# Attention and two expert layers on one core: first keys loaded once, and TensorE's hand-over matmuls of the set-up written a step earlier

## The chip, the core and the metric

The kernel runs on one core of a Trainium2 chip. A core has five engines that each take their instructions in the order in which they are written and wait for one another by semaphores: TensorE (PE in the profile; PEld its weight loads), VectorE (DVE), ScalarE (ACT), GpSimd (POOL) and Sync (SP), which here issues loads and stores. The metric is the device time of one execution in microseconds.

## The reference

Three layers follow one another: attention over pooled keys and values, a product layer, and a layer of eight experts with one chosen per token.

```python
k_p = k.reshape(B, H, Sp, pool, D).mean(axis=3)       # pool = 8; 8 x 8 heads, 576 x 64
v_p = v.reshape(B, H, Sp, pool, D).mean(axis=3)
scores = scale * np.matmul(q, k_p.transpose(0, 1, 3, 2))
...                                                   # softmax over the 72 pooled keys
return np.matmul(attn, v_p).astype(np.float32)
...
a = x @ w1                                            # 4608 tokens, 512 -> 1024
b = x @ w2
h = a * b @ w3
return (h @ w_out).astype(np.float32)
...
logits = x @ w_gate + modality_bias[modality_id]
h = np.maximum(x[mask] @ w1[e], 0.0)                  # mask: the tokens of expert e
out[mask] = gate_w[mask, None] * (h @ w2[e])
```

## The kernel before

**Precision.** The weights come as 64-bit numbers. A *conversion* of a piece (`step(n)`, L401) makes two 32-bit parts of it: ScalarE takes the next piece apart (`conv_a`, L391 and L393) and rounds the high part of this one (L408), VectorE puts the bits of the next one together (`conv_b`, L398 and L399), and GpSimd subtracts (`sub_pool`, L117) for the low part. A product is made of three matmuls (`mm3`, L112 to L114): high by high, high by low, low by high. Results of attention are split in the same way: ScalarE copies the high part out of PSUM, VectorE subtracts.

**Set-up** (`set_up`). The product of w3 and w_out (with the gate's weights worked in as extra columns) is made once, in two passes of eight *folds* (`fold_mm`, twelve matmuls each). A loop over rounds j = 0 to 7 makes the first pass: two conversions, then a fold. In rounds 2 to 5 it also writes the attention scores of one tile of 128 tokens: score matmuls (L263), VectorE's maxima and differences (L275, L277), the exponential on ScalarE, the sums and the normalisation. The keys pooled for it (`prep_k`, L177) come in through `load_k`. The second loop, again of eight folds, has one conversion for each fold and, by a table of hooks that run behind the fold (`more`), the first half's way out of PSUM, the sums of the values (`V1`), the transposes of the attention weights (`T`), their product with the values (`V`), and the gate's weights: `turn` transposes them, `mul` multiplies, `back` transposes the result and stores it as columns 256 to 259.

**First chunk** (`first_chunk`, chunk 0 of 9). `mm1` runs over m = 0 to 7: 24 matmuls against w1 and w2, then a times b on ScalarE and VectorE. Hooks with a key `(m,)` run before that product of a and b, hooks with key m behind it. They hold the conversions of the weights of m + 2, the scores of the next chunk, and the second half's gate. `mm_w` (L629) follows. From the second chunk on `next_chunk` runs, which has no conversions.

All engines' instructions are issued in the order of the code. PSUM has buffers by tag: four for `mm`, two for `tp`, one pair for `sc`; a matmul into a buffer waits until the last reader of what stood there is done. SBUF tiles go by tags in the same way (`st2` has two).

Of the kernel before, what the change touches and what calls it, by code (L numbers as in the profile page):

```python
# [22 lines left out]
P = 128  # L23
# [64 lines left out]
def _program(outer, tc, nc, I, out):  # L88
# [159 lines left out]
    def softmax_parts(t):  # L248
# [43 lines left out]
        return exps, norm, (ex, ext)  # L292

    def attn_T(exs, j, ps_of, t):
        if j < 4:
# [3 lines left out]
            nc.scalar.copy(t[:, 0], ps)  # L299
            nc.vector.tensor_tensor(t[:, 1], ps, t[:, 0].bitcast(F32), op=ALU.subtract)  # L300
            return t
        kn, lo = slice(0, 6 * TK), slice(2 * TK, 4 * TK)
        for n in range(2):
# [3 lines left out]
            nc.scalar.copy(t[kn, n], ps[kn])  # L307
            nc.vector.tensor_tensor(t[lo, n], ps[lo], t[lo, n].bitcast(F32), op=ALU.subtract)
        return t

    def attn_V(a, z, aT, xh, xl, ps_of):
        kn = slice(0, 6 * TK)
        for pr in range(4):
# [3 lines left out]
            nc.scalar.copy(xh[:, pr, a:z], ps)  # L317
            nc.vector.tensor_tensor(xl[:, pr, a:z], ps, xh[:, pr, a:z].bitcast(F32), op=ALU.subtract)
# [8 lines left out]
    aT0 = []  # L327

    class Attention:
# [19 lines left out]
        def S(self, i):  # L349
            self.K(i)  # L350
            for f in self.S3(i):
                f()

        def S3(self, i):
# [5 lines left out]

        def T(self, js):
            for j in js:
                t = aT0[j] if self.ch == 0 and j < 4 else st4("aT", (P, 2, 512), F32R)
                self.aT[j] = attn_T(self.ex, j, mm_ps if self.ch == 0 else tp_ps, t)
# [6 lines left out]
        def V(self):  # L371
            if not self.segs:
                return
# [3 lines left out]
            attn_V(a, z, self.aT, *self.x, mm_ps)  # L377
            if self.segs:
                need(prep_v2, self.segs[0][2])

# [92 lines left out]
    def w_gate(W, wf, ps_of):  # L473

        wT = {}
        g = []

        def turn(nb):
            tps = ps_of("wtp")
            for k in range(4):  # L480
                nc.tensor.transpose(tps[:, P * k:P * k + P], wf[:, k, P * nb:P * nb + P], ident)
            wT[nb] = st2("wT")
            nc.scalar.copy(wT[nb], tps)

        def mul(nb):
            if nb == 0:
                g.append(ps_of("wgp"))
            nc.tensor.matmul(g[0][:E], lhsT=wg[:, nb], rhs=wT[nb], start=nb == 0, stop=nb == 3)

        def back():  # L490
            gT = st2("gT", (E, 512))
            nc.scalar.copy(gT, g[0][:E])
            gp = ps_of("wgt")[:, :32].rearrange("p (k a b) -> p k a b", k=4, a=2)
            for k in range(4):
                nc.tensor.transpose(gp[:, k].rearrange("p a b -> p (a b)"), gT[:, P * k:P * k + P], ident[:E, :E])
            nc.scalar.copy(W[0][:, :, :, 256:260], gp)
            nc.vector.tensor_tensor(W[1][:, :, :, 256:260], gp, W[0][:, :, :, 256:260].bitcast(F32), op=ALU.subtract)
        return turn, mul, back
# [6 lines left out]
    def set_up():  # L505
# [497 lines left out]
```

## Time and profile before

| | us |
|---|---|
| median of 3 runs | 1357.05 |
| lowest, highest | 1353.14, 1358.21 |
| the profiled execution | 1350.23 |
| its span | 1348.5 |
| TensorE busy | 1234.3 (92%) |
| VectorE, GpSimd, ScalarE busy | 677.7, 402.3, 369.7 |

The profile is of one execution. Times in it count from the start of the span; the busy time of an engine is the time in which it had an instruction in work. Matmuls are pipelined: the distance between two starts is what one costs, not its own duration. The granted clock is 1.00 where TensorE has 2.4 GHz; over a stretch it is a mean between its two levels, 1.2 and 2.4 GHz.

### The profile page before, as it was taken

The page shows a single profiled execution, that of the slowest core. Times are in us where ns is not written, and L with a number is a line of the kernel's source. Part 1 is how long each engine was busy: PE and PEld are TensorE (multiplying, and loading weights), DVE is VectorE, ACT ScalarE, POOL GpSimd, SP SyncE. Part 2 cuts the span into 40 slices and gives each one's busy share as a digit, 9 for nine tenths or more (in the row PEclk, how much of TensorE's full clock was granted, in tenths as well). Part 3 has the DMA queues.
Part 4 walks back from the last instruction along what each step waited for, and adds up shares of the span by engine and source line. Part 5 has one row for each costly group of instructions (what it writes and reads, how often), then busy time and mean ns, then how long its engine had stood idle before and what let it go on. Part 6 is the DMA issues. An engine that isn't in the chain of part 4 may idle for free. (4 is left out here: it accounts for less than half of the span.)

```text
span 1348.5 us, 17452 instructions
## 1 busy us (share of the span) xinstructions
PE 1234.3 (92%) x6518; PEld 1046.4 (78%) x6518; DVE 677.7 (50%) x1325; ACT 369.7 (27%) x717; POOL 402.3 (30%) x464
## 2 busy tenths in 40 slices
PE   1566777799999999999999999999999999999997
PEld 1454546788989898898989889797888888888886
DVE  3574466554454545445453443465635565565452
ACT  2353454222222232323223222222121122212121
POOL 1361134014050231405023110314533443344142
PEclk8887888899999999999999999999999999999999
DMA  8502243130301203030020100224513441443240
GB/s 342 175 21 83 78 127 116 44 118 16 111 31 60 82 15 118 11 113 29 25 83 13 36 1 32 94 95 154 190 63 148 172 159 54 172 172 119 102 167 20
DMA packets 53165, 126.71 MB, mean 94 GB/s; under 512 B 12656, under 2 KB 12912, under 8 KB 53040
## 3 DMA queue, kind: packets, MB, share of 16 engines
q1 hardware_dynamic: 45680, 105.63, 22.5%
q0 software_dynamic: 7232, 19.71, 3.7%
q8 instruction: 57, 0.93, 0.3%
q14 instruction: 52, 0.43, 0.1%
q10 hardware_dynamic: 144, 0.02, 0.0%
HBM read 105.36 MB, written 20.55 MB: 93 GB/s over the span
## 5 line engine op out<-in xcount | busy, mean ns | idle before, releaser
L112 PE MATMUL w<-xh,w 128*128 128x512 f32 x576 | 231.8, 402 | 4.8 <-ACT w L408 1.9
L114 PE MATMUL w<-xh,w 128*128 128x512 f32 x576 | 227.2, 394 | 1.4 <-POOL w L117 1.4
L113 PE MATMUL w<-xl,w 128*128 128x512 f32 x576 | 226.4, 393 | 0.0
L289 POOL TENSOR_TENSOR ex<-ex,sm 128x576 f32<-128x576 f32 x36 | 41.7, 1159 | 391.2 <-PE sc L263 263.6
L112 PEld LDWEIGHTS w<-xh,w 128*128 128x128 f32 x576 | 109.6, 190 | 28.0 <-DVE asb L613 2.1
L114 PEld LDWEIGHTS w<-xh,w 128*128 128x128 f32 x576 | 109.3, 190 | 26.2 <-POOL w L117 2.7
L112 PE MATMUL e<-xh,e1h 128*128 128x512 f32 (+2 forms) x320 | 121.5, 380 | 5.7 <-issue 4.6
L113 PEld LDWEIGHTS w<-xl,w 128*128 128x128 f32 x576 | 109.7, 190 | 21.2
L113 PE MATMUL e<-xl,e1h 128*128 128x512 f32 (+2 forms) x320 | 122.6, 383 | 0.0
L114 PE MATMUL e<-xh,e1l 128*128 128x512 f32 (+2 forms) x320 | 121.1, 378 | 0.1
L114 PE MATMUL e<-e2h,abl 128*128 128x512 f32 x296 | 117.1, 395 | 3.0 <-DVE abl L813 3.0
L112 PE MATMUL e<-e2h,abh 128*128 128x512 f32 x296 | 117.8, 398 | 0.5 <-DVE abl L813 0.5
L629 PE MATMUL x2ps<-Wh,abh 128*128 128x260 f32 x576 | 118.2, 286 | 0.0
L629 PE MATMUL x2ps<-Wl,abh 128*128 128x260 f32 x576 | 116.7, 283 | 0.0
L113 PE MATMUL e<-e2l,abh 128*128 128x512 f32 x296 | 116.1, 392 | 0.0
L629 PE MATMUL x2ps<-Wh,abl 128*128 128x260 f32 x576 | 116.0, 283 | 0.0
L613 DVE TENSOR_TENSOR asb<-asb,w 128x512 f32<-128x512 f32 x72 | 49.3, 684 | 114.1 <-PE w L114 63.5
L614 ACT CAST abh<-asb 128x512 fp32r<-128x512 f32 x72 | 44.7, 620 | 182.8 <-DVE asb L613 182.8
L812 ACT ACTIVATE abh<-e 128x512 fp32r<-128x512 f32 (+2 forms) x80 | 45.4, 567 | 168.2 <-PE e L114 142.2
L825 POOL DMA_INDIRECT out<-o,idc x37 | 37.5, 1014 | 180.3 <-ACT o L824 166.9
L629 PEld LDWEIGHTS x2ps<-Wh,abh 128*128 128x128 f32 x576 | 89.9, 190 | 0.3
L629 PEld LDWEIGHTS x2ps<-Wl,abh 128*128 128x128 f32 x576 | 89.8, 189 | 0.0
(187 smaller groups left out, 2216.3 us busy)
## 6 DMA issues: line engine op xcount, KB each, us to landing
raw<-ew_in SPq DMA_DIRECT2D x80, 512.0 KB
q<-q_in SPq DMA_DIRECT2D x36, 256.0 KB
x2d<-x SPq DMA_DIRECT2D x36, 256.0 KB
kr<-k_in SPq DMA_DIRECT2D x28, 288.0 KB
vr<-v_in SPq DMA_DIRECT2D x28, 256.0 KB
cv<-w_in SPq DMA_DIRECT2D x12, 512.0 KB
stage<-w_in SPq DMA_DIRECT2D x10, 512.0 KB
stage<-wo_in SPq DMA_DIRECT2D x6, 512.0 KB
```

The lines of the kernel that those rows point to most:

```text
L112: nc.tensor.matmul(ps, lhsT=wh, rhs=xh, start=start, stop=False)
L113: nc.tensor.matmul(ps, lhsT=wh, rhs=xl, start=False, stop=False)
L114: nc.tensor.matmul(ps, lhsT=wl, rhs=xh, start=False, stop=stop)
L289: nc.gpsimd.tensor_tensor(e3, e3, bc(sm.unsqueeze(2), [P, H, SP_]), op=ALU.mult)
L613: nc.vector.tensor_tensor(a, a, ps[1], op=ALU.mult)
L614: nc.scalar.copy(abh[:, m], a)
L629: nc.tensor.matmul(pss[hf][:, :260], lhsT=l[:, m, cols], rhs=r[m // 4][:, m % 4, hf], start=m == 0 and r is Wh and l is abh, stop=m == 7 a ...
L812: nc.scalar.activation(hT[0][:, m, :w], ps[:, :w], AF.Relu)
L825: nc.gpsimd.indirect_dma_start(out=out, out_offset=bass.IndirectOffsetOnAxis(idc[:, i, 0:1], 0), in_=o, in_offset=None, bounds_check=N - 1 ...
```

## The change

The keys of batch 0 are remembered, so `prep_k(0)` doesn't load them a second time. In the set-up and the first chunk the small matmuls whose results another engine then reads (scores, transposes of attention and of the gate's weights, product with the values, the gate's products) are taken apart from the reading part (`diff`, `split`, `keep`, `out`) and stand a round, a fold or a step ahead of it: `parts(j - 1)` writes the score matmuls ahead of fold j, and their maxima follow in round j + 1. In the second pass the tables `vec` (the reading parts) and `ten` (TensorE's parts) both run ahead of the fold. The four turns of the second half's gate get a PSUM buffer each (two of `tp`, two banks of `sc`) and SBUF tiles of the tag `raw`. Sums of the values and loads of chunk 1 stand one or two steps earlier in m.

```diff
-        if b == 0:
+        if b == 0 and b not in k_raw:
             kr = ab0["abh"].bitcast(F32)[:, :4 * S].rearrange("p (a s) -> p a s", a=4)
             for pr in range(4):
                 nc.sync.dma_start(kr[:, pr], I["k"][b, :, pr * S:(pr + 1) * S])
                 if pr == 0:
                     load_q(0)
-            return [kr[:, pr] for pr in range(4)]
+            k_raw[0] = [kr[:, pr] for pr in range(4)]
...
-        for v, m, e, sh in parts:
-            nc.vector.tensor_reduce(out=m, in_=v, op=ALU.max, axis=AX.X)
-        for v, m, e, sh in parts:
-            nc.vector.tensor_tensor(e, v, bc(m.unsqueeze(len(sh) - 1), sh), op=ALU.subtract)
+        def diff():
+            for v, m, e, sh in parts:
+                nc.vector.tensor_reduce(out=m, in_=v, op=ALU.max, axis=AX.X)
+            for v, m, e, sh in parts:
+                nc.vector.tensor_tensor(e, v, bc(m.unsqueeze(len(sh) - 1), sh), op=ALU.subtract)
...
+        def split(to, of, part):
+            nc.scalar.copy(to, of)
+            nc.vector.tensor_tensor(part[0], part[1], part[2].bitcast(F32), op=ALU.subtract)
...
+            return lambda: split(t[:, 0], ps, (t[:, 1], ps, t[:, 0]))
...
-        def S3(self, i):
+        def parts(self, i):
...
+        def T2(self, js):
+            steps = []
+            for j in js:
+                t = self.aT[j] = aT0[j] if self.ch == 0 and j < 4 else st4("aT", (P, 2, 512), F32R)
+                steps.append(attn_T(self.ex, j, mm_ps if self.ch == 0 else tp_ps, t))
+            return steps
...
-            wT[nb] = st2("wT")
-            nc.scalar.copy(wT[nb], tps)
...
+        def keep(nb):
+            wT[nb] = wt_of()
+            nc.scalar.copy(wT[nb], tps[nb])
...
+            g.append(st2("gT", (E, 512)))
+            nc.scalar.copy(g[1], g[0][:E])
+
+        def back2():
+            gp = ps_of[5]("wgt")[:, :32].rearrange("p (k a b) -> p k a b", k=4, a=2)
+            g.append(gp)
...
+        def out():
+            nc.scalar.copy(W[0][:, :, :, 256:260], g[2])
+            nc.vector.tensor_tensor(W[1][:, :, :, 256:260], g[2], W[0][:, :, :, 256:260].bitcast(F32), op=ALU.subtract)
...
-        s3 = None
+        sm = {}
         for j in range(8):
-            if 2 <= j < 6:
-                att.K(j - 2)
-                s3 = att.S3(j - 2)
+            now = sm.get(j - 2)
+            if now:
+                now[0]()
             step(2 * j)
-            if s3:
-                s3[0]()
+            if now:
+                now[1]()
             step(2 * j + 1)
-            if s3:
-                s3[1]()
-            s3 = None
-            fold_mm(accs, j)
+            if now:
+                now[2]()
             if j == 0:
                 att.K(0)
                 raw_load(11)
                 load_v0()
+            if 1 <= j < 5:
+                sm[j - 1] = att.parts(j - 1)
+            fold_mm(accs, j)
...
-        more = {0: [lambda: fold_out(accs, W[0], wf0, (0, 1))],
-                1: [lambda: fold_out(accs, W[0], wf0, (2, 3)), lambda: att.V1()],
-                2: [lambda: att.T((0, 1))],
-                3: [lambda: att.T((2, 3)), lambda: load_k(1)],
-                4: [lambda: att.T((4,)), lambda: turn(0), lambda: turn(1)],
-                5: [att.V, lambda: mul(0), lambda: mul(1)],
-                6: [lambda: turn(2), lambda: turn(3)],
-                7: [lambda: mul(2), lambda: mul(3), back]}
+        late = []
+        def end():
+            for f in late:
+                f()
+            late[:] = []
+        vec = {0: [lambda: fold_out(accs, W[0], wf0, (0, 1))], 1: [lambda: fold_out(accs, W[0], wf0, (2, 3))],
+               2: [end, lambda: att.V1()], 3: [end, lambda: load_k(1)], 4: [end, lambda: keep(0), lambda: keep(1)],
+               5: [end], 6: [lambda: keep(2), lambda: keep(3)]}
+        ten = {1: [lambda: late.extend(att.T2((0, 1)))], 2: [lambda: late.extend(att.T2((2, 3)))],
+               3: [lambda: late.extend(att.T2((4,))), lambda: turn(0), lambda: turn(1)],
+               4: [lambda: late.extend(att.V(True))],
+               5: [lambda: turn(2), lambda: turn(3), lambda: mul(0), lambda: mul(1)],
+               7: [lambda: mul(2), lambda: mul(3)]}
         for j in range(8):
             step(16 + j)
+            run(vec, j)
+            run(ten, j)
             fold_mm(accs2, j)
-            run(more, j)
         step(24)
+        back()
+        back2()
         step(25)
+        w_out()
...
+        sc2 = psum.tile([P, 2, 512], F32, name="wtp2", tag="sc", bufs=1)
+        bank = lambda i: lambda name: sc2[:, i]
+        gate = w_gate(W[1], wf1, [tp_ps, tp_ps, bank(0), bank(1), tp_ps, tp_ps],
+                      lambda: at.tile([P, 512], F32, name="wT", tag="raw", bufs=RAW))
...
-        turn, mul, back = gate
-        s3 = []
+        turn, keep, mul, back, back2, w_out = gate
+        sm = {}
         def scores(i):
             att.K(i)
-            s3[:] = att.S3(i)
-
-        h1 = {(m,): [lambda m=m: step(28 + 2 * m), lambda m=m: step(29 + 2 * m)] for m in range(6)}
+            sm[i] = att.parts(i)
+        h0 = {m: [lambda m=m: step(28 + 2 * m), lambda m=m: step(29 + 2 * m)] for m in range(6)}
+        h1 = {m: [] for m in range(8)}
+        h0[0][:0] = [lambda: turn(0), lambda: turn(1), lambda: turn(2), lambda: turn(3)]
+        h0[0].insert(5, lambda: need(prep_k, 1))
+        h1[0] += [lambda: keep(0), lambda: keep(1), lambda: keep(2), lambda: keep(3)]
+        h0[1][:0] = [lambda: mul(0), lambda: mul(1), lambda: mul(2), lambda: mul(3)]
+        h1[1] += [back, lambda: load_k(2)]
+        h0[2][:0] = [back2]
+        h1[2] += [w_out]
         for i in range(4):
-            h = h1[i + 1,]
-            h.insert(0, lambda i=i: scores(i))
-            h.insert(2, lambda: s3[0]())
-            h.append(lambda: s3[1]())
-        h1[(0,)].insert(0, lambda: need(prep_k, 1))
-        h1[0] = [lambda: turn(0), lambda: turn(1)]
-        h1[1] = [lambda: mul(0), lambda: mul(1), lambda: turn(2), lambda: turn(3)]
-        h1[2] = [lambda: mul(2), lambda: mul(3), lambda: load_k(2)]
-        h1[3] = [back]
-        h1[4] = [load_routing]
-        h1[5] = [lambda: early_v(1), prep_routing]
-        h1[6] = [att.V1, lambda: att.T((0, 1))]
-        h1[7] = [lambda: att.T((2, 3)), lambda: att.T((4,))]
+            h0[i + 1].insert(len(h0[i + 1]) - (2 if i == 0 else 4), lambda i=i: scores(i))
+            h1[i + 1] += [lambda i=i: sm[i][0]()]
+            h0[i + 2].insert(len(h0[i + 2]) - 1, lambda i=i: sm[i][1]())
+            h0[i + 2] += [lambda i=i: sm[i][2]()]
+        h1[4] += [load_routing, lambda: early_v(1)]
+        h0[6] = [prep_routing]
+        h1[5] += [att.V1]
+        h1[6] += [lambda: att.T((0, 1))]
+        h1[7] += [lambda: att.T((2, 3)), lambda: att.T((4,))]
+        h1.update({(m,): h for m, h in h0.items()})
         ab = mm1(0, x, h1)
```

On TensorE, first pass: wps are the accumulators of the folds, f4 and f0 the operands of folds 0 and 1, f5 and f1 those of folds 2 and 3, and sc and scm the scores of tiles 0 and 1. Before:

```order
L114 MATMUL wps_146<-f4_108,f0_104 128x512
L263 MATMUL sc_233<-kblk0_87,q_121 128x144 x4
L112 MATMUL wps_143<-f5_109,f1_105 128x512
...
L114 MATMUL wps_146<-f5_109,f1_105 128x512
L263 MATMUL scm_279<-kblk0_87,q_129 128x144 x2
L263 MATMUL scm_280<-kblk0_87,q_129 128x144 x2
```

After:

```order
L114 MATMUL wps_146<-f4_108,f0_104 128x512
L263 MATMUL sc_217<-kblk0_87,q_121 128x144 x4
L112 MATMUL wps_143<-f4_108,f0_104 128x512
...
L263 MATMUL scm_263<-kblk0_87,q_129 128x144 x2
L263 MATMUL scm_264<-kblk0_87,q_129 128x144 x2
L112 MATMUL wps_143<-f5_109,f1_105 128x512
```

The scores of tile 0 stood behind folds 0 and 1 and now stand behind fold 0; those of tile 1 stood behind fold 2 and now stand behind fold 1, and so on up to tile 3. VectorE's order in these rounds is the same in both.

On TensorE, second pass: f_108, f_109 and f_110 belong to folds 0 and 1, 2 and 3, 4 and 5; atp are the transposes of the attention weights (the last ones from ext), wtp those of the gate's weights. Before:

```order
L114 MATMUL wps_482<-f_109,f_105 128x512
L298 MATMUL atp<-c,ex 128x128 x8
L112 MATMUL wps_480<-f_110,f_104 128x512
...
L114 MATMUL wps_482<-f_110,f_104 128x512
L306 MATMUL atp<-c,ext 96x128 x8
L481 MATMUL wtp<-c,earlyabh 128x128 x8
```

After:

```order
L114 MATMUL wps_478<-f_108,f_104 128x512
L305 MATMUL atp<-c,ex 128x128 x8
L112 MATMUL wps_476<-f_109,f_105 128x512
...
L114 MATMUL wps_478<-f_109,f_105 128x512
L312 MATMUL atp<-c,ext 96x128 x8
L500 MATMUL wtp<-c,earlyabh 128x128 x8
```

The second group of transposes moved from behind fold 3 to the place ahead of fold 2, and the last one, with the first two turns, from behind fold 4 to the place ahead of fold 3.

On TensorE, first chunk: w_865 and w_862 are the second accumulators of m = 0, w_923 and w_932 the first ones of m = 1, wf the second half's weights for the gate, wgp the gate's product. Before:

```order
L114 MATMUL w_865<-xh,w_797 128x512
L481 MATMUL wtp<-c,wf 128x128 x8
L112 MATMUL w_923<-xh,w_831 128x512
...
L263 MATMUL sc<-kblk_87,q 64x144 x4
L263 MATMUL sc<-kblk_88,q 64x144 x4
L488 MATMUL wgp<-wT,wg 8x512 x2
L481 MATMUL wtp<-c,wf 128x128 x8
```

After:

```order
L114 MATMUL w_862<-xh,w_784 128x512
L500 MATMUL wtp<-c,wf 128x128 x8
L500 MATMUL wtp_846<-c,wf 128x128 x8
L112 MATMUL w_932<-xh,w_827 128x512
...
L509 MATMUL wgp<-wT,wg 8x512 x4
L263 MATMUL sc<-kblk_87,q 64x144 x4
L263 MATMUL sc<-kblk_88,q 64x144 x4
```

All four turns now follow m = 0 and all four products follow m = 1, ahead of the scores; before, two turns and two products each stood one step of m apart.

## Rows read from the trace of the kernel before

**Rows 1.** Stretches: busy us of each engine (x instructions), TensorE's clock, DMA share, GB/s.

```profile
0.00:159.20 159.20, 89.41 (x292) 61.92 (x292) 76.55 (x103) 61.17 (x111) 47.87 (x52) 0.81 0.40 145
159.20:262.00 102.80, 75.37 (x343) 59.56 (x344) 63.40 (x101) 46.38 (x87) 31.40 (x28) 0.85 0.30 97
262.00:362.00 100.00, 100.00 (x645) 91.57 (x645) 46.26 (x110) 27.95 (x64) 20.37 (x34) 1.00 0.21 68
10.00:20.00 10.00, 5.52 (x12) 3.60 (x12) 2.35 (x2) 4.62 (x8) 2.57 (x2) 1.00 1.03 418
```

**Rows 2.** TensorE's waits from 262 to 860 us: total, times, longest.

```profile
PE rps L666 <- DVE r_oh L659: 0.2, 1, 0.2
```

**Rows 3.** Timeline to 34 us: start, us, engine, line, [idle before <- releaser].

```profile
18.07 4.04 SPq L161 DMA_DIRECT2D earlyabh<-k_in  x4
...
27.47 2.88 DVE L177 TENSOR_REDUCE ks<-earlyabh 128x72 f32<-128x576 f32 x4 [12.70 <-DMA earlyabh<-k_in]
...
33.24 0.80 PE L112 MATMUL wps<-f,f 128*128 128x512 f32 x1 [14.66 <-ACT f L408]
```

**Rows 4.** VectorE's waits from 36 to 75 us.

```profile
DVE mx L275 <- PE sc L263: 9.9, 2, 6.4
DVE mx L275 <- PE scm L263: 5.9, 2, 3.0
DVE scr L398 <- ACT scr L393: 2.3, 4, 0.6
```

**Rows 5.** Timeline of one round, VectorE and GpSimd.

```profile
50.13 0.95 DVE L275 TENSOR_REDUCE mx<-scm 128x4 f32<-128x288 f32 x2 [2.98 <-PE scm L263]
...
52.44 0.69 DVE L399 SCALAR_TENSOR_TENSOR scr<-scr 128x512 int32<-128x512 int32 x1
...
54.46 1.66 DVE L399 SCALAR_TENSOR_TENSOR scr<-scr 128x512 int32<-128x512 int32 x1
...
57.02 0.20 DVE L286 RECIPROCAL sm<-sm 128x8 f32<-128x8 f32 x1
...
58.94 1.28 POOL L117 TENSOR_TENSOR f<-scr,f 128x512 fp32r<-128x512 f32 x1
```

**Rows 6.** Timeline of the second pass, TensorE and ScalarE.

```profile
91.86 0.39 PE L112 MATMUL wps<-f,f 128*128 128x512 f32 x1
...
92.09 0.39 PE L113 MATMUL wps<-f,f 128*128 128x512 f32 x1
...
100.30 0.91 ACT L231 ACTIVATE vbh<-vs,c 128x256 fp32r<-128x256 f32 x2 [4.62 <-POOL vs L146]
...
111.51 0.50 PE L112 MATMUL wps<-f,f 128*128 128x512 f32 x1 [2.35 <-ACT f L408]
...
159.23 0.50 PE L112 MATMUL w<-xh,w 128*128 128x512 f32 x1 [1.89 <-ACT w L408]
```

**Rows 7.** Timeline of the first chunk, TensorE and two rows of VectorE.

```profile
175.20 1.74 PE L263 MATMUL sc<-kblk,q 128*64 128x144 f32 x16
...
179.35 1.94 PE L488 MATMUL wgp<-wT,wg 128*8 128x512 f32 x4 [2.42 <-ACT wT L483]
...
188.97 0.78 PE L112 MATMUL w<-xh,w 128*128 128x512 f32 x1
...
197.20 0.76 DVE L275 TENSOR_REDUCE mx<-sc 128x8 f32<-128x576 f32 x1 [8.82 <-PE sc L263]
...
206.03 0.75 DVE L275 TENSOR_REDUCE mx<-sc 128x8 f32<-128x576 f32 x1
...
214.09 0.59 PE L495 MATMUL wgt<-c,gT 8*128 8x8 f32 x4 [8.45 <-ACT gT L492]
...
236.54 0.50 PE L112 MATMUL w<-xh,w 128*128 128x512 f32 x1 [1.19 <-ACT asb L612]
...
248.68 1.97 PE L298 MATMUL atp<-c,ex 128*128 128x128 f32 x8 [6.41 <-DVE aT L300]
...
253.44 0.78 PE L629 MATMUL x2ps<-Wh,abh 128*128 128x260 f32 x2
```

More of the change, by code (lines that the diff above doesn't have):

```diff
@@ L306, in attn_T, with attn_V @@
                 nc.tensor.transpose(ps[kn, P * i:P * i + P], ext[:, n].rearrange("p d q k -> p (d q k)"), ident)
[L307 to L311, printed above, removed]
+            steps.append(lambda n=n, ps=ps: split(t[kn, n], ps[kn], (t[lo, n], ps[lo], t[lo, n])))
+        return lambda: [f() for f in steps]
+    def attn_V(a, z, aT, xh, xl, ps_of, late=False):
         kn = slice(0, 6 * TK)
+        steps = []
         for pr in range(4):
@@ L316, in attn_V, with split @@
             nc.tensor.matmul(ps, lhsT=vbt[kn, pr], rhs=aT[4][kn, pr // 2, a:z], start=False, stop=True)
-            nc.scalar.copy(xh[:, pr, a:z], ps)
-            nc.vector.tensor_tensor(xl[:, pr, a:z], ps, xh[:, pr, a:z].bitcast(F32), op=ALU.subtract)
+            def split(pr=pr, ps=ps):
+                nc.scalar.copy(xh[:, pr, a:z], ps)
+                nc.vector.tensor_tensor(xl[:, pr, a:z], ps, xh[:, pr, a:z].bitcast(F32), op=ALU.subtract)
+            steps.append(split)
+            if not late:
+                split()
+        return steps
     done = set()
@@ L350, in S @@
             self.K(i)
-            for f in self.S3(i):
+            for f in self.parts(i):
                 f()
-        def S3(self, i):
+        def parts(self, i):
             *steps, ex = softmax_parts(4 * self.ch + i)
@@ L359, in S3 @@
             return steps
+        def T2(self, js):
+            steps = []
+            for j in js:
+                t = self.aT[j] = aT0[j] if self.ch == 0 and j < 4 else st4("aT", (P, 2, 512), F32R)
+                steps.append(attn_T(self.ex, j, mm_ps if self.ch == 0 else tp_ps, t))
+            return steps
         def T(self, js):
             for j in js:
-                t = aT0[j] if self.ch == 0 and j < 4 else st4("aT", (P, 2, 512), F32R)
-                self.aT[j] = attn_T(self.ex, j, mm_ps if self.ch == 0 else tp_ps, t)
+                for f in self.T2([j]):
+                    f()
         def V1(self):
@@ L369, in V1, with V @@
             need(prep_v2, self.segs[0][2])
-        def V(self):
+        def V(self, late=False):
             if not self.segs:
-                return
+                return []
             if self.x is None:
@@ L376, in V @@
             a, z, b = self.segs.pop(0)
-            attn_V(a, z, self.aT, *self.x, mm_ps)
+            steps = attn_V(a, z, self.aT, *self.x, mm_ps, late)
             if self.segs:
                 need(prep_v2, self.segs[0][2])
+            return steps
     def load64(src, raw):
@@ L540, in set_up @@
                 load_v0()
+            if 1 <= j < 5:
+                sm[j - 1] = att.parts(j - 1)
+            fold_mm(accs, j)
         W = [product(0)]
         wf0 = ab0["abh"].bitcast(F32)[:, :2048].rearrange("p (k n) -> p k n", k=4)
-        turn, mul, back = w_gate(W[0], wf0, mm_ps)
+        turn, keep, mul, back, back2, w_out = w_gate(W[0], wf0, [mm_ps] * 6, lambda: st2("wT"))
         sc = psum.tile([P, 2, 512], F32, name="wps3", tag="sc", bufs=1)
@@ L566, in set_up @@
         step(27)
-        return att.x, ([w[0] for w in W], [w[1] for w in W]), w_gate(W[1], wf1, tp_ps)
+        sc2 = psum.tile([P, 2, 512], F32, name="wtp2", tag="sc", bufs=1)
+        bank = lambda i: lambda name: sc2[:, i]
+        gate = w_gate(W[1], wf1, [tp_ps, tp_ps, bank(0), bank(1), tp_ps, tp_ps],
+                      lambda: at.tile([P, 512], F32, name="wT", tag="raw", bufs=RAW))
+        return att.x, ([w[0] for w in W], [w[1] for w in W]), gate
     mi = cst.tile([P, NT], I64, name="mi")
```

26 lines of the change are left out of this document (9 added, 17 removed).

## Prediction

> **What bounds the kernel now.** I read the table by stretches first. From 262 us on TensorE is busy all the time at a granted clock of 1.00; before that it is busy 89.4 of 159.2 us and 75.4 of 102.8 us, at mean clocks of 0.81 and 0.85 [rows 1]. The list of waits says the same for the long middle: between 262 and 860 us TensorE waits 0.2 us in all [rows 2]. So the middle has no slack and its length doesn't change; a change of the set-up and the first chunk moves everything behind it by what it takes out before the first matmul of L629, at 253.44 us [rows 7]. Then I read the timeline of these 253 us, engine by engine. The reader is to see the same shape again and again: an engine waits for TensorE to get past a whole fold to the small matmul written behind it, and TensorE then waits for the conversion that this engine does next.
>
> I call the second pass's folds 0 to 7 and count the chunk's steps m from the first matmul of m = 0, at 159.23 us [rows 6]. The profiled execution took 1350.23 us (span 1348.5); the median of the three runs is 1357.05, 6.8 us more. I make the sum against the profiled one and move the forecast up by that 6.8.
>
> **A. The second load of the keys, -12.7 us.** Sync issues the keys among its first loads (the third to the seventh, with one q between) and again, four loads, at 18.07 us into the same tile. VectorE's first reduction over them starts at 27.47 us after 12.70 us of idling for that DMA, so VectorE was free at 14.77 [rows 3]. Without the second load it waits for the first only. Ahead of the first load's end lie two weight pieces of 512 KB, one q of 256 and four key pieces of 288, 2.4 MB; at the 418 GB/s of 10 to 20 us [rows 1] that is 6 us, so they are there by about 10 us. All behind them moves with VectorE: the fold that began at 33.24 us [rows 3] begins at about 20.6. Bounds: 12.7 if the data is there at 14.77; 2.8 (1.18 MB less at 418 GB/s) if the queue were what is waited for. I take 12.7. The ring piece that Sync loads behind the reductions, and the values behind it, go out earlier by the same amount, so no later weight piece is later than before.
>
> **B. Scores a round ahead, -13.7 us.** In rounds 2 to 5 VectorE starts with the maxima of the scores, and waits for them 9.9 and 5.9 us, four waits, 15.8 us [rows 4]: the score matmuls stand behind the previous fold. After, they stand ahead of it, and the tile read in a round was made a fold earlier, so I take all 15.8 away. What is late next is VectorE itself. One round's work runs from 50.13 to 57.22 us (57.02 + 0.20), 7.1 us. In the idle time GpSimd made the other half of a split, at 58.94 us; after, that lands on the conversions. L399 takes 0.69 us alone and 1.66 us beside GpSimd [rows 5], so a meeting costs 1.0 to 1.3 us; the 0.6 us that VectorE waited for ScalarE in a round [rows 4] goes, as ScalarE gets ahead meanwhile. I take 0.7 a round for the three rounds that follow one another: 15.8 - 2.1 = 13.7. Bounds: 15.8 with no meeting, 10 with two more meetings a round. The cover of the score matmuls themselves is VectorE's 7.8 us a round; the fold takes 12 x 0.23 to 0.46 (below) = 2.8 to 5.5 us.
>
> The Trainium skill, "SBUF — State Buffer", section "Who interferes with whom", says that a VectorE instruction with two SBUF inputs contends with a GpSimd one that reads SBUF, and that one fully blocks the other. Row L399 agrees (1.66 against 0.69 us). By that rule a round can't be shorter than VectorE's four conversions plus all GpSimd work of the round, some 7 us as an estimate, so B could gain at most 2.4 us more.
>
> **C. Second pass, -23 us.** Its first fold begins at 91.86 us, the last stretch ends at 159.23 [rows 6]: 67.4 us. Folds 0 to 3: little. The value sums stay on GpSimd and ScalarE still waits for them (4.62 us, to 100.30 us) before the next conversion; they now come one conversion later, some 3.7 us by the same rows' order. New is a wait: the turns of the gate's weights (L481) are written ahead of fold 3 and need PSUM buffers that VectorE frees only after that conversion. I follow it from the row at 100.30, as an estimate: ScalarE's values (0.91 and a smaller pair) and its half of a conversion 2.5, VectorE's half 0.69 + 1.66 [rows 5], one split of that size 0.7, hand-overs 0.2, so +5.8; turns +1.1; fold 3 at 100.30 + 3.7 + 6.9 = 110.9 against 111.51 now [rows 6]: 0.6 us gained. From fold 3 on TensorE has all inputs ahead: five folds x 12 matmuls x 0.23 us (91.86 to 92.09 [rows 6]) = 13.8, V 16 x 0.23 = 3.7, four gate products at 1.94 the pair [rows 7] = 3.9, turns 1.0 and 0.4 for the way back: 22.8 us at 2.4 GHz, twice that at 1.2. The stretch now has a clock of 0.81, which is 38% of the time at the lower level; as TensorE stands less I take 20%, 22.8 / 0.9 = 25.3 us, against 159.23 - 111.51 = 47.7. C = 0.6 + 22.4 = 23. Bounds: 25.5 all at 2.4 GHz; 3 all at 1.2.
>
> **D. First chunk, -18 us.** Its end, 253.44, is 94.2 us behind m = 0. VectorE's first product and the copies of the turned weights aren't touched: the gate products begin 20.1 us in (179.35 [rows 7]), and now all four stand there (3.9 us), then the scores (1.74, at 175.20 now [rows 7]): m = 2 at 25.7 us, against 29.7 (188.97). That is 4 us. From there to m = 7 it takes 47.6 us now (236.54), with 8.45 us of waiting for the gate's way back, since that stands behind a whole step of ScalarE; after, VectorE's period bounds: 8.8 us (197.20 to 206.03 [rows 7]), against TensorE's 24 x 0.23 + 1.74 = 7.3 at most. Four such periods and a short one, 38 us: 9.5 gained. The end, 16.9 us, holds a wait of 6.41 us for VectorE [rows 7], which sums values then; these sums are moved two steps ahead, I take 4.5. D = 18. Bounds 10 to 22.
>
> **Sum.** 12.7 + 13.7 + 23 + 18 = 67: 1350.2 - 67 = 1283, and 1290 as a median. What I cost at nothing: one issue order on every queue otherwise; the next chunk's loads behind the keys of chunk 2, which now wait for the gate products (23.9 us into the chunk) while the weights behind them are wanted some 20 us later.
>
> **Rivals.** (1) *Half of it.* The clock stays low and the meetings on VectorE and GpSimd are dearer: B 10, C 5 to 12, D 10 to 12: gain 38 to 47, 1310 to 1319. For it: 0.81 and 0.85 in these stretches; against it: TensorE's stops are what goes. (2) *Slower.* TensorE takes its work in order, and hand-over matmuls ahead of a fold hold that fold until PSUM buffers come free. The wait ahead of fold 3 is such a one: buffers free at +5.8 us, TensorE done with fold 2 about 5 us sooner. If one of 5 us came at each of the 8 folds and 8 steps, 80 us would go against 67: 1370. It decides from 67 / 16 = 4.2 us a place. Against it: elsewhere four buffers were freed a step before. (3) *No change.* The set-up's end is set by something else, the weights' arrival: 1357. Against it: the list of what VectorE waits for from 36 to 75 us names TensorE and ScalarE and no load [rows 4]. (4) *The keys' wait only changes its name* (the next piece isn't there): A 2.8, 1300.
>
> **Chances.** The sum as worked out, 1279 to 1302, rival 4 in it: 0.66. Rival 1: 0.28. Rival 2: 0.03. Rival 3: 0.03. The range leaves out the last two and the ends of the first two: low 1279 (C all at 2.4 GHz, D 22, B 15.8), high 1318. Faster by over 0.5%, about what a measurement of this kernel tells from none: 0.94; within: 0.03; slower: 0.03.
>
> **What would show it.** Keys once in the list of issues, the reduction at 14.8 us; the waits of L275's counterpart for TensorE gone in rounds 2 to 5, a period near 7.8 us; a wait of some 5 us ahead of fold 3; m = 0 near 110 us, the first matmul of L629's counterpart near 186. A new wait of TensorE ahead of most folds would make me wrong, as would a clock below 0.8 from fold 3 on.

## The result, and the profile after

The changed kernel takes 1283.14 us (median of four runs, 1282.17 to 1283.80) against 1355.30 for the kernel before (1353.14 to 1358.21); the ratio is 0.9466, 95% interval 0.9443 to 0.9488. It is 72 us faster; the forecast was 1290 in a range of 1279 to 1318.

The table by stretches answers to [rows 1]: busy time of PE, PEld, DVE, ACT and POOL with their instructions, TensorE's clock, DMA share, GB/s.

```profile
0.00:159.20 159.20, 119.27 (x502) 88.02 (x503) 122.03 (x166) 97.53 (x177) 79.48 (x73) 0.91 0.52 184
159.20:262.00 102.80, 96.28 (x555) 84.85 (x554) 54.85 (x120) 30.15 (x62) 25.32 (x41) 0.97 0.22 71
82.50:107.60 25.10, 25.10 (x102) 17.55 (x101) 15.90 (x19) 13.95 (x27) 7.07 (x5) 0.95 0.47 168
```

In the first 159.2 us TensorE is now busy for 119.3 us instead of 89.4, and the granted clock is 0.91 instead of 0.81; the second stretch went from 0.85 to 0.97. These windows no longer hold the same work, since the set-up now ends at 106.66 us. By the work, the clock went from 0.81 to 0.90 in the set-up and from 0.86 to 0.92 in the first chunk. The third row is the second pass from fold 3 on, in which TensorE never stops.

The timeline of set-up and first chunk answers to [rows 3], [rows 5], [rows 6] and [rows 7]: start, duration, engine, line, [idle before <- releaser]. L276, L419, L500, L509 and L672 are L275, L399, L481, L488 and L629 of before.

```profile
14.70 2.72 DVE L177 TENSOR_REDUCE ks<-earlyabh 128x72 f32<-128x576 f32 x4
...
20.31 0.50 PE L112 MATMUL wps<-f,f 128*128 128x512 f32 x1 [0.85 <-ACT f L428]
...
34.52 0.70 DVE L276 TENSOR_REDUCE mx<-sc 128x8 f32<-128x576 f32 x1
...
39.15 1.64 DVE L419 SCALAR_TENSOR_TENSOR scr<-scr 128x512 int32<-128x512 int32 x1
...
41.82 0.77 DVE L276 TENSOR_REDUCE mx<-scm 128x4 f32<-128x288 f32 x2
...
63.27 0.39 PE L112 MATMUL wps<-f,f 128*128 128x512 f32 x1
...
75.27 0.91 ACT L231 ACTIVATE vbh<-vs,c 128x256 fp32r<-128x256 f32 x2 [5.58 <-POOL vs L146]
...
80.92 1.97 PE L500 MATMUL wtp<-c,earlyabh 128*128 128x128 f32 x8 [6.64 <-DVE f L300]
82.54 0.78 PE L112 MATMUL wps<-f,f 128*128 128x512 f32 x1
...
106.66 0.50 PE L112 MATMUL w<-xh,w 128*128 128x512 f32 x1
...
126.61 4.96 PE L509 MATMUL wgp<-wT,wg 128*8 128x512 f32 x8 [6.16 <-ACT wT L504]
...
133.17 0.50 PE L112 MATMUL w<-xh,w 128*128 128x512 f32 x1
...
177.27 1.97 PE L305 MATMUL atp<-c,ex 128*128 128x128 f32 x8 [4.39 <-DVE aT L300]
...
182.03 0.78 PE L672 MATMUL x2ps<-Wh,abh 128*128 128x260 f32 x2
```

The rows give the four parts of the gain. The keys' reduction starts at 14.70 instead of 27.47 us, and fold 1 at 20.31 instead of 33.24: 12.9 us. The second pass begins (63.27) 28.6 us earlier than at 91.86, so the scores gave 15.7. From there to m = 0 it takes 43.4 instead of 67.4 us: 24.0. From m = 0 (106.66) to the first matmul of L672 (182.03; called *the mark* from here on) it takes 75.4 instead of 94.2: 18.8. In all the mark is 71.4 us earlier.

VectorE's waits from 20 to 75 us, which answer to [rows 4], name TensorE no more; those for ScalarE stayed:

```profile
DVE scr L418 <- ACT scr L413: 2.6, 5, 0.5
DVE Wl L491 <- ACT earlyabh L490: 2.1, 2, 1.8
```

TensorE's waits from 186 to 850 us, as [rows 2] of a longer stretch before:

```profile
PE w L112 <- DVE asb L656: 2.5, 1, 2.5
PE rps L709 <- DVE r_oh L702: 0.2, 1, 0.2
```

The middle still has no slack; the 2.5 us are one wait at its end, 1.7 before. Behind the mark the profiled execution took 1281.2 - 182.0 = 1099.2 us, against 1348.5 - 253.4 = 1095.1 before: 4.1 us of the 71.4 were given back there. TensorE's wait for VectorE at the first expert's second product is 5.8 us in this trace and 2.6 in that of before; `after_again` and `w1_vector` below are about it.

### The profile page after: what moved, and what is told of

It reads as the page before. It is cut to its first block, busy times and chain, and to the rows that moved or that the text cites. A ratio compares the mean times of both kernels' runs of the same rounds, so it can differ in the third digit from the quotient of the medians.

```text
span 1281.2 us, 17451 instructions
## 1 busy us (share of the span) xinstructions
PE 1213.8 (95%) x6518; PEld 1035.1 (81%) x6518; DVE 678.2 (53%) x1325; ACT 370.0 (29%) x717; POOL 407.6 (32%) x464
## 5 line engine op out<-in xcount | busy, mean ns | idle before, releaser
L112 PEld LDWEIGHTS w<-xh,w 128*128 128x128 f32 x576 | 108.2, 188 | 24.2 <-DVE asb L656 2.9
L114 PEld LDWEIGHTS w<-xh,w 128*128 128x128 f32 x576 | 108.1, 188 | 24.1 <-POOL w L117 1.1
L672 PE MATMUL x2ps<-Wh,abh 128*128 128x260 f32 x576 | 118.0, 286 | 0.0
L672 PE MATMUL x2ps<-Wl,abh 128*128 128x260 f32 x576 | 116.4, 283 | 0.0
L672 PE MATMUL x2ps<-Wh,abl 128*128 128x260 f32 x576 | 115.8, 282 | 0.0
L672 PEld LDWEIGHTS x2ps<-Wh,abh 128*128 128x128 f32 x576 | 89.7, 189 | 0.3
L672 PEld LDWEIGHTS x2ps<-Wl,abh 128*128 128x128 f32 x576 | 89.5, 189 | 0.0
```

The costliest lines, as they stand in the source:

```text
L112: nc.tensor.matmul(ps, lhsT=wh, rhs=xh, start=start, stop=False)
L114: nc.tensor.matmul(ps, lhsT=wl, rhs=xh, start=False, stop=stop)
L672: nc.tensor.matmul(pss[hf][:, :260], lhsT=l[:, m, cols], rhs=r[m // 4][:, m % 4, hf], start=m == 0 and r is Wh and l is abh, stop=m == 7 a ...
```

## The experiments

Since the stretch behind the mark turned out to differ by up to 7 us from trace to trace, each run is read at the mark as well as by its time. Three traces of the same code have the mark at 182.03, 182.28 (`after_again`) and 182.77 us (`w1_vector`), so it is read to some 0.7 us. The first four were timed beside the kernel before at 1353.04 us, the next four beside 1351.27, the last three beside 1352.45.

**One part alone, and three parts undone.** `a_alone` is the kernel before with these lines:

```diff
-        if b == 0:
+        if b == 0 and b not in k_raw:
...
-            return [kr[:, pr] for pr in range(4)]
+            k_raw[0] = [kr[:, pr] for pr in range(4)]
```

> The kernel before, with the keys of batch 0 remembered and nothing else changed. Theory (the parts add up, and the second load alone held VectorE): VectorE's first reduction of the keys starts at about 14.7 us instead of 27.47, the second fold at about 20.4 instead of 33.24, and all behind it is 12.7 us earlier: 1355.3 - 12.7 = 1342.6 us. Rival (the weights are what is waited for next): the reduction starts early, but the folds of the first pass wait for conversions whose loads aren't there, and less than half of it is left, 1350 us or more.

Measured: 1340.07 us, ratio 0.9899 (0.9874 to 0.9924), so 13.0 us less. Its timeline:

```profile
15.07 2.72 DVE L177 TENSOR_REDUCE ks<-earlyabh 128x72 f32<-128x576 f32 x4
...
20.68 0.50 PE L112 MATMUL wps<-f,f 128*128 128x512 f32 x1 [2.08 <-ACT f L408]
...
243.47 0.78 PE L629 MATMUL x2ps<-Wh,abh 128*128 128x260 f32 x2
```

The second load alone held VectorE: the data is there at 15.07, and fold 1 is 12.6 us earlier. The next three folds are 11.7, 11.2 and 10.9 us earlier and the mark 10.0: some 2.6 us are lost again, most of them in the rounds in which VectorE and TensorE still wait for one another; why there, isn't settled. The rival, which leaves less than half, is out.

`b_undone` is the changed kernel with the score matmuls behind the fold again:

```diff
-            now = sm.get(j - 2)
-            if now:
-                now[0]()
+            now = None
+            if 2 <= j < 6:
+                att.K(j - 2)
+                now = att.parts(j - 2)
+                now[0]()
...
+            fold_mm(accs, j)
             if j == 0:
...
-            if 1 <= j < 5:
-                sm[j - 1] = att.parts(j - 1)
-            fold_mm(accs, j)
```

> The changed kernel, with the score matmuls of the first pass put back to the start of the round that reads them, behind the fold before (keys once, second pass and first chunk as changed). Theory: VectorE waits again for the score matmuls in four rounds, 15.8 us in all by the trace before; the second pass's first fold starts at about 79 us instead of 63.3, and the time is 1283.1 + 15.8 = 1299 us. Rival (the waits in the second pass have slack that takes it up, since the value sums need only VectorE and GpSimd): 1290 us or less.

Measured: 1293.40 us, ratio 0.9577 (0.9550 to 0.9604). The timeline:

```profile
27.32 0.76 DVE L276 TENSOR_REDUCE mx<-sc 128x8 f32<-128x576 f32 x1 [6.37 <-PE sc L263]
...
198.45 0.78 PE L672 MATMUL x2ps<-Wh,abh 128*128 128x260 f32 x2
```

VectorE's waits are back, and the mark is 16.4 us later than in the changed kernel, as the theory has it; nothing in the second pass took it up. The time rose by 10.3 us only, because this trace has 1092.3 us behind the mark.

`c_undone` puts the second pass's hooks back behind the folds:

```diff
         for j in range(8):
             step(16 + j)
-            run(vec, j)
-            run(ten, j)
             fold_mm(accs2, j)
+            run(more, j)
...
```

> The changed kernel, with the second pass's hooks behind each fold in the order and places of the kernel before, the reading part right behind TensorE's part. Theory: from the second pass's first fold to the first matmul of m = 0 it takes 67.4 us again instead of 43.4, so 24 us more: 1307 us. Rival (the part is smaller by itself, because the first chunk as changed is bound by VectorE and waits less when it starts later): 1295 to 1300 us.

Measured: 1307.71 us, ratio 0.9672 (0.9643 to 0.9700), 24.6 us above the changed kernel. In its timeline folds 2 to 5 and 7 wait 2.3 to 5.7 us again (folds 2 and 3 are shown), and the mark is 26.2 us later:

```profile
74.80 0.79 PE L112 MATMUL wps<-f,f 128*128 128x512 f32 x1 [5.65 <-ACT f L428]
...
83.02 0.50 PE L112 MATMUL wps<-f,f 128*128 128x512 f32 x1 [2.35 <-ACT f L428]
...
208.23 0.78 PE L669 MATMUL x2ps<-Wh,abh 128*128 128x260 f32 x2
```

`d_undone` gives the first chunk its old hooks and the gate its old buffers:

```diff
-        gate = w_gate(W[1], wf1, [tp_ps, tp_ps, bank(0), bank(1), tp_ps, tp_ps],
-                      lambda: at.tile([P, 512], F32, name="wT", tag="raw", bufs=RAW))
+        gate = w_gate(W[1], wf1, [tp_ps] * 6, lambda: st2("wT"))
...
+        h1[0] = [lambda: tk(0), lambda: tk(1)]
+        h1[1] = [lambda: mul(0), lambda: mul(1), lambda: tk(2), lambda: tk(3)]
+        h1[2] = [lambda: mul(2), lambda: mul(3), lambda: load_k(2)]
+        h1[3] = [bk]
```

> The changed kernel, with the first chunk's hooks and the buffers of the second half's gate as before. Theory: from the first matmul of m = 0 to the first one of the product with the folded weights it takes 94.2 us again instead of 75.4, so 18.8 us more: 1302 us. Rival (the parts depend on one another, the old chunk ran slow only because the clock was low when it began): under 10 us more, 1292 us or less.

Measured: 1297.65 us, ratio 0.9603 (0.9576 to 0.9630), 14.5 us above the changed kernel; the mark is 16.7 us later. Both stops of the gate are there again, although the chunk is entered as in the changed kernel: m = 0 at 106.92 us, and a granted clock of 1.00 in the 6.9 us ahead of it (the kernel before has 0.75 in the 9.2 us ahead of its chunk). So the old order makes them, and a low clock at the start isn't needed (`tk` is turn and copy in one, `bk` the whole way back):

```profile
133.64 1.11 PE L500 MATMUL wtp<-c,wf 128*128 128x128 f32 x4 [6.33 <-ACT wT L504]
...
159.00 0.59 PE L519 MATMUL wgt<-c,gT 8*128 8x8 f32 x4 [8.45 <-ACT gT L513]
...
198.69 0.57 PE L669 MATMUL x2ps<-Wh,abh 128*128 128x260 f32 x1
```

At the mark the four parts are 10.0 (alone) and 16.4, 26.2 and 16.7 (undone), 69.3 of 71.4 us: they add up to all but 2.1 us. Part by part the two readings differ by up to 2.9 us (A is 12.9 us in the changed kernel and 10.0 alone).

**The two new stops.** TensorE now waits 6.64 us ahead of fold 3 and 6.16 ahead of the gate's products. `turns_later` takes the turns, which wait, from fold 3; their copies (`keep`) move with them:

```diff
...
-               3: [lambda: late.extend(att.T2((4,))), lambda: turn(0), lambda: turn(1)],
+               3: [lambda: late.extend(att.T2((4,)))],
                4: [lambda: late.extend(att.V(True))],
-               5: [lambda: turn(2), lambda: turn(3), lambda: mul(0), lambda: mul(1)],
+               5: [lambda: turn(0), lambda: turn(1)],
+               6: [lambda: turn(2), lambda: turn(3), lambda: mul(0), lambda: mul(1)],
```

> The changed kernel, with the four turns of the first half's gate, their copies and the first two products two folds, or one, later in the second pass; nothing stands ahead of fold 3 but the last transposes of the attention weights. Theory (the stop ahead of fold 3 is really the value sums': GpSimd ends them at 75.2 us, ScalarE and VectorE do the next conversion and the halves of the split only then): fold 3 may start some 3 us earlier, but the product with the values behind it waits for the split that ends at 84.9 us, so 1.6 us are gained at most, 1281.5 us. Rival (the turns' wait for PSUM is what costs): the 6.6 us come back, 1276.5 us.

Measured: 1276.62 us, ratio 0.9455 (0.9441 to 0.9469). By the time the rival has it, almost to the number that it named; the timeline says otherwise:

```profile
78.72 0.80 PE L112 MATMUL wps<-f,f 128*128 128x512 f32 x1 [4.13 <-ACT f L428]
...
180.57 0.78 PE L673 MATMUL x2ps<-Wh,abh 128*128 128x260 f32 x2
```

Fold 3 starts 3.8 us earlier and still waits 4.13, now for ScalarE's conversion. The mark moved by 1.5 us, as the theory has it; the other 5 us are the stretch behind the mark (1093.9 us here), and the ratio's interval overlaps that of the changed kernel.

`sums_early` spreads the value sums over three places from the end of the first pass on (`vsums[i]` is one sum on GpSimd and one on VectorE):

```diff
+            if j == 7:
+                vsums = sums0()
+                vsums[0]()
...
-        vec = {0: [lambda: fold_out(accs, W[0], wf0, (0, 1))], 1: [lambda: fold_out(accs, W[0], wf0, (2, 3))],
+        vec = {0: [vsums[1], lambda: fold_out(accs, W[0], wf0, (0, 1))], 1: [vsums[2], lambda: fold_out(accs, W[0], wf0, (2, 3))],
```

> The changed kernel, with the sums of the values of batch 0 taken apart and written behind the last conversion of the first pass and the first two of the second, one on GpSimd and one on VectorE each, instead of all behind the third. Theory (the value sums set the stop ahead of fold 3): ScalarE's wait of 5.58 us for GpSimd goes, the stop shrinks from 6.6 to about 1.5 us and all behind moves up by 5 us: 1278 us. Rival (GpSimd's subtraction for the next folds comes later instead, since the sums now lie ahead of it): 1282 to 1284 us, with a wait of TensorE for GpSimd at the first folds of the second pass.

Measured: 1273.49 us, ratio 0.9423 (0.9408 to 0.9437). ScalarE's row of 75.27 us stands at 69.53, without a wait, and the stop shrank:

```profile
69.53 0.98 ACT L243 ACTIVATE vbh<-vs,c 128x256 fp32r<-128x256 f32 x2
...
76.87 1.39 PE L512 MATMUL wtp<-c,earlyabh 128*128 128x128 f32 x8 [2.60 <-DVE f L312]
...
177.44 0.78 PE L687 MATMUL x2ps<-Wh,abh 128*128 128x260 f32 x2
```

The mark is 4.6 us earlier: GpSimd's sums set that stop, and the turn was only the instruction at which TensorE met it. The rival, a wait of the next folds for GpSimd, didn't come.

`keys_early` pools the keys of batch 1 in the second pass:

```diff
-               5: [end], 6: [lambda: keep(2), lambda: keep(3)]}
+               5: [end], 6: [lambda: keep(2), lambda: keep(3), lambda: need(prep_k, 1)]}
...
-        h0[0].insert(5, lambda: need(prep_k, 1))
```

> The changed kernel, with the pooling of the keys of batch 1 (VectorE, 3.4 us at 120.00 us) moved from the first chunk's step m = 0 to the second pass, behind the conversion at 92 us, where VectorE idles for 3.13 us. Theory (the first chunk is bound by VectorE from m = 0 to its last transposes): 3.4 us less, 1279.7 us. Rival (ScalarE's copies of the turned weights and TensorE set the step): no change, 1283 us.

Measured: 1274.17 us, ratio 0.9429 (0.9416 to 0.9443). The reduction lies where VectorE idled, and from m = 0 (105.11) to the mark it takes 71.5 instead of 75.4 us, 3.9 less:

```profile
92.97 2.72 DVE L177 TENSOR_REDUCE ks<-kr 128x72 f32<-128x576 f32 x4
...
121.63 3.60 PE L509 MATMUL wgp<-wT,wg 128*8 128x512 f32 x8 [2.73 <-ACT wT L504]
...
176.59 0.78 PE L672 MATMUL x2ps<-Wh,abh 128*128 128x260 f32 x2
```

The theory is right for the chunk. Another 1.5 us came from ahead of the edit and are not its own: fold 4, which begins ahead of the moved reduction, is as much earlier. TensorE's wait ahead of the gate's products shrank along with it, from 6.16 to 2.73 us, because ScalarE's copies follow VectorE's product of m = 0.

`gate_early` also moves the copies of the turned weights:

```diff
-        h1[0] += [lambda: keep(0), lambda: keep(1), lambda: keep(2), lambda: keep(3)]
+        h0[0][5:5] = [lambda: keep(0), lambda: keep(1), lambda: keep(2), lambda: keep(3)]
```

> The same as the run before it in this list (keys of batch 1 pooled in the second pass), and ScalarE's four copies of the turned weights right behind the first conversion of m = 0, instead of behind the product of a and b. Theory: TensorE's wait of 6.16 us ahead of the gate's products goes, but VectorE still sets the pace, so that the steps behind it wait for VectorE's product of a and b two steps before; VectorE starts its next conversion 2 us earlier, so 3.4 + 2.1 = 5.5 us less than the changed kernel: 1277.6 us, with TensorE waiting some 4 us longer for VectorE later in the chunk. Rival (TensorE's wait was the cost): 3.4 + 6.2 = 9.6 us less, 1273.5 us.

Measured: 1273.84 us, ratio 0.9427 (0.9412 to 0.9441), the same as without this move; from m = 0 to the mark 72.1 us against 71.5. The 2.73 us that `keys_early` had left of TensorE's wait ahead of the products are gone. TensorE waits instead ahead of three scores, 4.4 us in all where `keys_early` has 1.9 and the changed kernel 0.8, and 4.83 us ahead of the last transposes, against 3.98 and 4.39. The list of waits names no releaser for the scores ("issue"), but each of them starts 0.1 us behind VectorE's last read of the scores before it (L278), as the first one here:

```profile
PE sc L263 <- issue: 4.4, 3, 1.8
...
131.96 0.76 DVE L278 TENSOR_TENSOR ex<-sc,mx 128x576 f32<-128x576 f32 x1
...
132.82 1.22 PE L263 MATMUL sc<-kblk,q 128*128 128x144 f32 x8 [1.10 <-issue]
...
141.35 1.22 PE L263 MATMUL sc<-kblk,q 128*128 128x144 f32 x8 [1.83 <-issue]
...
178.79 0.78 PE L672 MATMUL x2ps<-Wh,abh 128*128 128x260 f32 x2
```

So what was left of TensorE's wait was no cost by itself, and the larger part of it, 3.4 us, went with work that was taken off VectorE: VectorE sets this chunk. The theory's other half, 2.1 us from ScalarE, was wrong too: the copies now hold ScalarE ahead of the conversion before, VectorE's product of m = 0 comes 16.4 us into the chunk instead of 14.7 (in `keys_early`), and that of m = 1 at 22.5 instead of 22.7.

**All of it together.** `best` has `sums_early`, `turns_later` and `keys_early`, the routing's set-up behind the last transposes, and VectorE's maxima and differences in the gap in which it waits for ScalarE to round the product (0.69 us in each of eight steps):

```diff
             nc.scalar.copy(abh[:, m], a)
+            run(hooks, ("mid", m))
             nc.vector.tensor_tensor(abl[:, m], a, abh[:, m].bitcast(F32), op=ALU.subtract)
...
-            h1[i + 1] += [lambda i=i: sm[i][0]()]
+            h1["mid", i + 1] = [lambda i=i: sm[i][0]()]
...
-        h0[6] = [prep_routing]
...
-        h1[7] += [lambda: att.T((2, 3)), lambda: att.T((4,))]
+        h1[7] += [lambda: att.T((2, 3)), lambda: att.T((4,)), prep_routing]
```

> The changed kernel with five moves together: the value sums spread over three earlier places, the first half's turns later, the keys of batch 1 pooled in the second pass, the routing's set-up on VectorE behind the first chunk's last transposes, and in the steps m = 1 to 4 the maxima and differences of the scores between ScalarE's rounding of the product and VectorE's second half of it. Theory (VectorE's order sets the first chunk, GpSimd's value sums the stop ahead of fold 3): 4.9 + 1 us from the second pass, 3.9 for the keys, 2.4 for the routing, 4 x 0.69 = 2.8 for the gap: the first matmul of the product with the folded weights at about 167 us instead of 182.0, and with what follows it (1092 to 1099 us in the traces so far) and 2 us around the span 1261 to 1268 us. Rival (TensorE bounds the stretch once the stops are gone): under 8 us at that matmul, 1270 us or more.

Measured: 1263.22 us, ratio 0.9343 (0.9326 to 0.9360), faster than both kernels and 15.9 us below the changed kernel timed beside it (`after_again`). The mark is one us from what the sum gave, 16.0 us ahead of the changed kernel's; from m = 0 to it the chunk takes 67.6 us instead of 75.4:

```profile
98.41 0.50 PE L112 MATMUL w<-xh,w 128*128 128x512 f32 x1
...
166.03 0.78 PE L689 MATMUL x2ps<-Wh,abh 128*128 128x260 f32 x2
```

That the sum fits so well is in part luck: ahead of m = 0 it is 8.25 us where 5.9 were summed, as TensorE no longer stops ahead of fold 3 at all, and in the chunk 7.8 where 9.1 were. What the routing's set-up and the gap gave, each by itself, wasn't tried.

**Behind the mark.** `after_again` is the changed kernel a second time.

> The changed kernel itself, beside the kernels of this list. Theory (what follows the set-up varies between kernels by the luck of one chain of transfers, and for one kernel little): 1283 us again, the first matmul of the product with the folded weights at 182 us, 1099 us behind it, and TensorE's wait of 5 to 6 us at the first expert's second product. Rival (that wait varies from run to run): 1276 to 1283 us, with the wait anywhere between 1 and 6 us.

Measured: 1279.13 us, ratio 0.9472 (0.9449 to 0.9494). The mark is at 182.28, 0.25 us from the first trace, and behind it are 1095.0 us instead of 1099.2: the rival has it, the stretch behind the mark varies for one and the same kernel. VectorE's rows at the first expert's end, in the first trace, with TensorE's and GpSimd's beside them:

```profile
857.90 0.76 DVE L828 CAST e1h<-raw 128x512 fp32r<-128x512 f32 x2 [6.66 <-DMA raw<-ew_in]
...
859.38 3.71 DVE L828 CAST e1h<-raw 128x512 fp32r<-128x512 f32 x2
...
860.30 2.49 POOL L117 TENSOR_TENSOR e1l<-raw,e1h 128x512 fp32r<-128x512 f32 x2
...
863.00 0.68 DVE L862 SCALAR_TENSOR_TENSOR abl<-e,abh 128x512 fp32r<-128x512 f32 x1
...
863.73 0.80 PE L114 MATMUL e<-e2h,abl 128*128 128x512 f32 x1 [5.79 <-DVE abl L862]
```

And in the second, with the wait of TensorE from the list of waits (total, times, longest) below:

```profile
858.62 0.76 DVE L828 CAST e1h<-raw 128x512 fp32r<-128x512 f32 x2
859.29 0.68 DVE L862 SCALAR_TENSOR_TENSOR abl<-e,abh 128x512 fp32r<-128x512 f32 x1
859.89 3.07 DVE L830 TENSOR_TENSOR e1l<-raw,e1h 128x512 fp32r<-128x512 f32 x1
...
859.88 2.52 POOL L117 TENSOR_TENSOR e1l<-raw,e1h 128x512 fp32r<-128x512 f32 x2
...
PE e L114 <- DVE abl L862: 2.8, 1, 2.8
```

VectorE's order is the same in both: casts of the next group's weights, then the half of the product for which TensorE waits, then a subtraction. While GpSimd makes its two subtractions, one instruction of VectorE is held up for some 3 us: in the first trace the second of the two casts ahead of L862 (3.37 us instead of 0.42; TensorE waits 5.8 us), in the second the subtraction behind L862 (3.07 instead of 0.68; TensorE waits 2.8 us). The other traces bear it out. In three (the changed kernel, `keys_early`, `best`) the cast is held up, TensorE waits 5.1 to 5.8 us, and the first subtraction starts 0.9 us behind the start of the pair of casts. In eight it is VectorE's subtraction, TensorE waits 1.3 to 2.8 us, and the distance is 1.3 us. In `sums_early` it is 0.1 us, a single subtraction holds up the first cast (1.69 us), and TensorE waits 3.9 us. So a few tenths between two engines go with some 3 us of waiting. The Trainium skill, "SBUF — State Buffer", section "Who interferes with whom", says that a cast too can take the port pair that VectorE shares with GpSimd, if its operands meet certain conditions, that whoever issues first keeps the pair for the whole instruction, and that the other is fully blocked. The held cast agrees with the blocking, as it ends 0.3 us behind the second subtraction; its record starts 0.6 us ahead of the first one's, so these rows don't show who issued first.

This wait is 3.0 of the 4.2 us by which the two traces differ behind the mark, and the wait at the end of the middle (2.5 and 1.8 us) is another 0.7. It isn't the only cause of the spread: the eight traces with the short wait still have 1092.3 to 1097.4 us behind the mark, and what makes that difference stays open.

`w1_vector` takes GpSimd out of that place (`on_v` is true there alone):

```diff
-            if k:
+            if k or on_v:
                 nc.vector.tensor_tensor(l2, r, h2.bitcast(F32), op=ALU.subtract)
...
-            load_w1(nr[0])
+            load_w1(nr[0], late)
```

> The changed kernel, with the halves of the second expert group's first weights that GpSimd subtracts (eight pieces of 128 x 512) on VectorE instead, at that one place; the rest of the program is the same. Theory (VectorE's last half of the first expert's hidden values stands behind casts that GpSimd's subtraction holds up: 3.71 us instead of 0.76): TensorE's wait there falls from 5.8 to about 3.5 us, and the time by 2 to 3 us. Rival (the load of these weights sets the wait): the wait stays at 5 to 6 us, and VectorE's longer work adds 0 to 2 us.

Measured: 1277.75 us, ratio 0.9451 (0.9437 to 0.9466), 1.4 us below `after_again`, which the intervals don't tell apart. No cast there is held up any more, and the wait is 2.6 us. That doesn't show a gain, in the wait or in time: `after_again` has 2.8 us without the edit, and behind the mark this trace has 1279.0 - 182.8 = 1096.2 us, between the two of the changed kernel:

```profile
859.12 0.42 DVE L828 CAST e1h<-raw 128x512 fp32r<-128x512 f32 x1
859.45 0.68 DVE L862 SCALAR_TENSOR_TENSOR abl<-e,abh 128x512 fp32r<-128x512 f32 x1
...
PE e L114 <- DVE abl L862: 2.6, 1, 2.6
```

## Why the prediction was right, step by step

**What bounds the kernel.** That the middle follows the mark held to 4 us in 1095; what I didn't see is that its length varies by itself, in part with where GpSimd's subtractions fall.

**A**, forecast 12.7: 12.8 at the reduction, 12.9 at fold 1. The data was there at 14.7 us, the upper bound of the term; `a_alone` confirms it where the second load ends, and shows that without the other parts 2.7 us of it are lost again by the mark.

**B**, forecast 13.7: 15.7, and 16.4 by `b_undone`. The waits of 15.8 us went whole. The term that was mis-sized is the 0.7 us a round for GpSimd's meetings: a round takes 7.30 us (34.52 to 41.82), not 7.8, beside 7.1 of work before. The one meeting on L419 (1.64 us) was in a round of before already, as 1.66; the new one, on L418, costs 0.45 us (1.14 instead of 0.69) and not 1.3. The 0.6 us that VectorE waited for ScalarE in a round, which I let go, stayed: 0.5 us a round, 2.6 us in all. The bound that I worked out from the rule in the Trainium skill ("SBUF — State Buffer", section "Who interferes with whom"), some 7 us a round, was not broken.

**C**, forecast 23: 24.0, and 26.2 by `c_undone`. The new wait came where it was forecast, ahead of fold 3, with 6.64 us instead of about 5, and fold 3 gained 0.4 us instead of 0.6 against the pass's start. I put its cause down to the PSUM buffers and the conversion; the experiments show that the value sums on GpSimd, which I followed as the first link of that chain, are what can be taken away. From fold 3 on it took 24.1 us instead of 25.3, since the clock was 0.95 and not the 0.9 that I took.

**D**, forecast 18: 18.8, and 16.7 by `d_undone`; here the sum is better than its terms, and that is luck. The products start 19.95 us into the chunk (20.1), m = 2 at 26.5 (25.7, the products took 4.96 us instead of 3.9). The middle gave 13.6 us instead of 9.5, the end 2.0 instead of 4.5; the sums of the values had moved ahead by one step, not by the two that I wrote. The step that failed is "VectorE's period bounds" for TensorE's steps: VectorE's period is 8.3 us (its products of a and b at 141.27, 149.60 and 157.83), but TensorE ran its steps in 5.6 to 7.5 us, as PSUM's four buffers of `mm` allow it to run two steps ahead, and paid at the end, where it waits 4.39 and 1.20 us for VectorE. Bound by VectorE was right for the chunk (`keys_early`, `gate_early`), only not where it shows.

**The rivals.** Half of it: the clock rose to 0.90 in the set-up and 0.92 in the first chunk instead of staying low. Slower: two stops of over 6 us did come, each above the 4.2 us from which that rival decides if it is at all 16 places; they came at two, and taking away what was left of the second gained nothing (`gate_early`). No change, and the keys' wait that only changes its name: the reduction at 14.7 us and the mark exclude both.

**The number.** The median of before with a fourth run is 1355.3, 1.8 us less than the 1357.05 from which I started; the gain was 72.2 instead of 67, so 1283 instead of 1290. The sum for the profiled execution also gave 1283, and 1283.10 was measured; that this fits to a tenth is luck, as 71.4 us were gained at the mark and 4.1 given back behind it. The 6.8 us by which I moved the forecast up weren't there after the change, whose profiled execution is its median to 0.04 us. The low end of the range doesn't follow from the terms named for it, which give 1357 - 76 = 1281 and not 1279.

## What to carry to other kernels

TensorE takes its work in order, so the small matmul whose result another engine waits for belongs ahead of the long block, a step before it is read; here that gave some 58 of 71 us. Then look at what the stop's own wait hides: removing TensorE's stop gains only if no other engine sets the pace, and the engine that sets it is the one that the new waits are for. Where a stretch behind the change varies by itself, read an edit at a mark in the timeline ahead of that stretch; `turns_later` would have been read the wrong way round by its time.

## What was not expected of the hardware

Two casts of 128 x 512 on VectorE took 3.71 us beside two of GpSimd's subtractions, and 0.76 without, and two traces of the same kernel differ by 3 us in TensorE's wait at that place, by which of VectorE's instructions was held up. The chain ahead of that place begins on GpSimd: four indirect scatters, of which in the first trace the last three wait 3.0 to 3.4 us each for the one before to land; Sync waits 5.9 us for the last of them before it issues the loads that VectorE's casts and GpSimd's gathers wait for.
